# Value products in whole float32, the two heads of a pair on two column halves of the array

## The chip, the cores and the metric

The kernel runs on one core of a Trainium2 chip. The metric is the device time of one execution in microseconds (us). The engines are named as in the profile: PE (matrix products), PEld (its loads of the stationary operand), DVE (VectorE), ACT (ScalarE), POOL (GpSimd) and SP (SyncE, which issues the transfers).

## The reference

An attention with a threshold is followed by a gated MLP. B = 8 batches, H = 8 heads, S = 576 tokens, D = 64; the model width is 512, the MLP's inner width 1024.

```python
scores = scale * np.matmul(q, k.transpose(0, 1, 3, 2))
thresh = np.max(scores, axis=-1, keepdims=True) - tau
scores = np.where(scores >= thresh, scores, -1000000000.0)
attn = np.exp(scores - np.max(scores, axis=-1, keepdims=True))
attn = attn / (np.sum(attn, axis=-1, keepdims=True) + 1e-09)
x = np.matmul(attn, v)              # heads side by side: (B, S, 512)

h = gelu_tanh(x @ w_in)             # (B, S, 1024)
u, v = h[..., :512], h[..., 512:]
v_n = layer_norm(v) * g_ln
v_s = np.einsum('ts,bsd->btd', w_sg, v_n) + b_sg[None, :, None]
out = x + (u * v_s) @ w_out
```

All of it is float32.

## The kernel before

A pair of heads is the unit of attention: `attention(n, g0)` for n = 0 to 31, four pairs to a batch. `moe(b, m0)` is the MLP of one batch, and its steps are laid between those of the next batch's attention. The 576 tokens are four tiles of 128 and a tail of 64.

For one pair, nine tiles of scores are computed (four for each head, one with the tails of both). Each tile goes through the row maximum (`nm`, DVE, L771), the exponential (`exp`, ACT, L797), the selection by the threshold with the row sum (`stt`, DVE, L804), and four transposes on PE (`t`, L495), because the value products need the key tokens on the partitions. The query tokens are handled in two parts `p`, of 256 and 320 columns (`PARTS`).

Most products take both operands as a sum of two parts in the short format fp32r (hi and lo), which PE multiplies in one pass. For the value products of pairs n >= 4 this means:

- the transposed probabilities are copied out of their bank as `pth` by ACT (step `hi`, L886), and DVE subtracts that from the bank to get `ptl` (step `lo`, L892); the tails likewise (`thi` L911, `tlo` L918);
- the values are split by ACT (`v_hi`, L718) and POOL (`v_lo`, L722) into `vst`, in which the 128 columns of a weight tile hold the 64 hi and the 64 lo columns of one head;
- per head and part, `values_main` (steps `pva`, `pvb`, L933) and `values_tail` (`pvt`, `pvc`, L942) multiply five key tiles, each with hi and with lo, into a bank of their own;
- ACT copies the two halves of that bank out (`vl0`, `vl1`, L957 and L958), POOL adds them (`xadd`, L963) and multiplies by the reciprocal row sum (`rmul`, L971).

For the first four pairs (`WHOLE_VALUES = 4`, `whole_v` in the code) the values and probabilities are not split: the products run on float32 operands, with 128 weight columns that hold both heads' values, of which one half of the result is used (L955). The profile shows a float32 product as two instructions.

The result `x` is split into `xh` and `xl` for the MLP (`xh` ACT L975, `xl` POOL L979). The MLP's products are in `products` (L1050): `v`, `u`, `y` (the token mixing), `o`.

The order of all engines' work is one list. The kernel's body is first rehearsed by a `Planner`, which gives each operation a duration (`time_of`), simulates the engines, and writes the list. Each kind of step has a place in time, `OFF` and `START`, by which the planner chooses among the steps that could start. `LOOK` says per engine how far ahead it looks. Four PSUM banks (`b0` to `b3`) are given out by it as well; the scores have buffers of their own.

Of the kernel before, what the change touches and what calls it, by code (L numbers as in the profile page):

```python
# [20 lines left out]
P = 128  # L21
# [12 lines left out]
    tau=-10.43, q_tails=35.82, w_load=93.12, w_abs=-193.45, w_word=-6.26, w_mul=289.27, w_add=-517.97, w_hi=490.97,  # L34
    w_lo=88.35, w_cast=112.5, w_rest=110.21, w_place=-69.47, q_load=-19.53, q_scale=259.5, q_hi=-6.99, q_lo=142.39,
    q_place=-47.78, q_place_lo=-48.53, k_load=-7.75, k_hi=-106.32, k_lo=-457.88, k_place0=-35.09, k_place1=52.53,
    l_place0=5.62, l_place1=117.11, v_load=92.53, v_hi=397.22, v_lo=13.94, s=-1.81, nm=590.35, thr=-183.16,
    exp=181.68, stt=24.69, t=1.61, hi=2.32, lo=468.05, rep=76.71, tt=-25.16, thi=-43.36, tlo=71.94, guard=-110.37,
    recip=463.46, irep=-433.54, turn=-94.76, inv=154.09, pva=-176.92, pvt=-141.14, vl0=0.73, pvb=-23.65, pvc=1.45,
    vl1=63.24, xadd=-45.27, rmul=6.15, xh=629.7, xl=-44.57, pe=3.02, mcopy=10.33, msq=22.97, stt1=-7.91, tanh=4.97,  # L40
    stt2=-9.02, bn=17.0, ag=17.81, var=29.8, rstd=-93.73, shift=-18.7, vn=-147.62, z=-102.8, zh=-53.93, zl=-85.64,
    mg=-72.27, mgh=31.11, mgl=-83.38, mo=12.11, mxl=8.52, mxh=40.16, mst=6.76,
)
START = {
# [5 lines left out]
}  # L50
LAST_SCALE, SIGMA, SPREAD = 0.55, 1.155, 0.7
LOOK = dict(tensor=139.2, vector=19.4, scalar=59.9, gpsimd=0.0, sync=204.7)
# [3 lines left out]
WHOLE_SCORES, WHOLE_VALUES = 1, 4  # L56
# [22 lines left out]
def time_of(engine, op, out, args):  # L79
# [7 lines left out]
    if engine == "tensor":  # L87
        passes = 2 if op == "transpose" else 4 if args[0].dtype == F32 else 1
        return n * passes / (CLOCK if passes > 1 else STREAM) + 2
# [294 lines left out]
def tile_threshold_attention_gated_mlp(  # L384
# [21 lines left out]

    nc = tc.nc
# [76 lines left out]
    VB = 5 * P  # L484
    vst = cpool.tile([P, 2 * (VB + D)], F32R, name="vst")
    nc.gpsimd.memset(vst[D:P, NM * P:VB].bitcast(F32), 0.0)
    nc.gpsimd.memset(vst[0:D, VB + NM * P:2 * VB].bitcast(F32), 0.0)

# [123 lines left out]
    def attention(n, g0):  # L612
# [5 lines left out]
        whole_s, whole_v = n < WHOLE_SCORES, n < WHOLE_VALUES  # L618

        def load(name, src, w):  # L620
            if name == "v" and whole_v:
                pool, width, tag = xpool, S, f"x{'hl'[n % 2]}{4 + n // 2}"
            elif name != "v" and whole_s:
# [77 lines left out]
        def v_parts():  # L701
            r = st["v"]
            main = r[:, :2 * NM * D].rearrange("p (t h d) -> p h t d", t=NM, h=2)
            hi = vst[:, 0:2 * (VB + D)].rearrange("p (h x) -> p h x", h=2)[:, :, 0:NM * P]
            hi = hi.rearrange("p h (t x) -> p h t x", t=NM)[:, :, :, 0:D]
            lo = vst[:, D:D + 2 * (VB - D)].rearrange("p (h x) -> p h x", h=2)[:, :, 0:NM * P]
            lo = lo.rearrange("p h (t x) -> p h t x", t=NM)[:, :, :, 0:D]
            for h in range(2):
                yield main[:, h], hi[:, h], lo[:, h]
            for h in range(2):  # L710
                rows = slice(h * D, (h + 1) * D)
                o = h * VB + NM * P
                yield (r[rows, 2 * NM * D:S], vst[rows, o + h * D:o + h * D + D],
                       vst[rows, o + (1 - h) * D:o + (1 - h) * D + D])

        def v_hi():
            for src, hi, _ in v_parts():
                nc.scalar.activation(hi, src, AF.Copy)  # L718

        def v_lo():  # L720
            for src, hi, lo in v_parts():
                nc.gpsimd.tensor_tensor(lo, src, hi, ALU.subtract)  # L722

        def v_tail_room():
            t = st["vt"] = ptp.tile([P, P], F32, tag="ttl", name=f"vt{n}")
            for h in range(2):
                nc.gpsimd.memset(t[h * D:(h + 1) * D, (1 - h) * D:(2 - h) * D], 0.0)

        def v_tail():
            for h in range(2):  # L730
                rows = slice(h * D, (h + 1) * D)
                nc.scalar.activation(st["vt"][rows, rows], st["v"][rows, 2 * NM * D:S], AF.Copy)
# [118 lines left out]
        parts = [("h", F32)] if whole_v else [("h", F32R), ("l", F32R)]  # L851

        def unit(h, p):
            if ("u", h, p) not in st:
                st["u", h, p] = tuple(
                    ptp.tile([P, NM, S - 2 * P], dt, tag=f"pt{x}{h}", name=f"pt{x}{n}_{h}_{p}") for x, dt in parts)
            return st["u", h, p]

        def tail_unit(p):
            if ("tu", p) not in st:  # L860
                st["tu", p] = tuple(
                    ptp.tile([P, S - 2 * P], dt, tag=f"tt{x}", name=f"tt{x}{n}_{p}") for x, dt in parts)
            return st["tu", p]
# [9 lines left out]
        def views(h, i):  # L873
            tp = st["t", h, i]
            if i < NM:
                p, j = divmod(i, 2)
                cs = slice(j * P, (j + 1) * P)
                return [(tp.rearrange("p (k x) -> p k x", k=NM), *(x[:, :, cs] for x in unit(h, p)))]
            src = tp.rearrange("p (k h x) -> p h k x", k=NM, h=2)
            cs = slice(2 * P, 2 * P + TAIL)  # L880
            return [(src[:, hh], *(x[:, :, cs] for x in unit(hh, 1))) for hh in range(2)]

        def hi_parts(h, i):
            def f():
                for src, hi, *_ in views(h, i):
                    nc.scalar.activation(hi, src, AF.Copy)  # L886
            return f

        def lo_parts(h, i):
            def f():  # L890
                for src, hi, lo in views(h, i):
                    nc.vector.tensor_tensor(lo, src, hi, ALU.subtract)  # L892
# [15 lines left out]
        def tail_hi(i):  # L908
            def f():
                p, cs, w = tail_place(i)  # L910
                nc.scalar.activation(tail_unit(p)[0][:, cs], st["tt", i][:, 0:w], AF.Copy)  # L911
            return f

        def tail_lo(i):
            def f():
                p, cs, w = tail_place(i)
                hi, lo = tail_unit(p)
                nc.vector.tensor_tensor(lo[:, cs], st["tt", i][:, 0:w], hi[:, cs], ALU.subtract)  # L918
            return f

        def value_tile(h, kt):

            if whole_v:
                return st["v"][:, kt * P:(kt + 1) * P] if kt < NM else st["vt"]
            return vst[:, h * VB + kt * P:h * VB + (kt + 1) * P]

        def values_main(h, p):
            def f():
                w = PARTS[p][1]
                acc = st["acc", h, p] = bank(f"pv{n}_{h}_{p}")  # L930
                for kt in range(NM):
                    for x, part in enumerate(unit(h, p)):
                        nc.tensor.matmul(acc[:, 0:w], value_tile(h, kt), part[:, kt, 0:w],  # L933
                                         start=(kt == 0 and x == 0), stop=False)
            return f

        def values_tail(h, p):
            def f():
                w = PARTS[p][1]
                tail = tail_unit(p)  # L940
                for x, part in enumerate(tail):
                    nc.tensor.matmul(st["acc", h, p][:, 0:w], value_tile(h, NM), part[:, 0:w],  # L942
                                     start=False, stop=(x == len(tail) - 1))
            return f

        def low_values(h, p):
            def f():
                w = PARTS[p][1]
                mine, other = slice(h * D, (h + 1) * D), slice((1 - h) * D, (2 - h) * D)
                if ("x", p) not in st:  # L950
# [360 lines left out]
```

## Time and profile before

| | |
|---|---|
| median of 3 runs | 1072.83 us (1068.9 to 1073.52) |
| profiled execution: its own time | 1072.98 us |
| profiled execution: span of its instructions | 1071.2 us |
| PE busy | 1012.8 us, 95% of the span, 6972 instructions |
| PEld busy | 934.3 us, 87% |
| DVE busy | 812.3 us, 76% |
| ACT busy | 815.5 us, 76% |
| POOL busy | 764.5 us, 71% |
| mean granted PE clock | 0.989 |
| transfers | 95.45 MB |

Busy time is the time in which an engine has at least one instruction under way. A product is pipelined: its own duration is longer than the step from its start to the next start, so the pace of PE is read from starts. In lists of groups a row reads: line, engine, operation, output<-inputs, shape, count, then busy time in us and mean duration in ns, then the idle time before the group and what ended it. In lists of waits a row reads: the waiting engine and line, what released it, then us in total, how many times, the longest.

### The profile page before, as it was taken

The numbers are of one execution on the slowest core, as the hardware profiler recorded it, in microseconds if no ns is written. First come the engines' busy times: TensorE is split into PE (matmuls) and PEld (weight loads), VectorE is DVE, ScalarE is ACT, GpSimd is POOL, SyncE is SP. The second block draws the span as 40 slices with busy tenths as digits, with TensorE's granted clock in tenths as the row PEclk, the third lists the DMA queues.
The fourth block names the chain that finished last, engine by engine and source line by source line (L and its number), as shares of the span: only waits on it lengthen the run. The fifth ranks groups of instructions, "written<-read, shape, count | busy, mean of one in ns | idle before, by whom it ended". The sixth has DMA issues, their size and how long they took to land.

```text
span 1071.2 us, 21247 instructions
## 1 busy us (share of the span) xinstructions
PE 1012.8 (95%) x6972; PEld 934.3 (87%) x6972; DVE 812.3 (76%) x1755; ACT 815.5 (76%) x1849; POOL 764.5 (71%) x1331
## 2 busy tenths in 40 slices
PE   4888899999999999999999999999999999999998
PEld 2667777998989988998989998999889999899987
DVE  5775778787887878887787878788787887878450
ACT  4777778877887788878787778878787788977662
POOL 6877767657975688757876588747886578864766
PEclk9898999999999999999999999999999999999999
DMA  9453332334232433334323442334333343331101
GB/s 287 132 134 87 86 71 55 93 93 113 66 98 69 102 94 91 81 81 103 100 63 92 98 108 65 98 82 109 82 83 92 87 104 91 76 86 24 40 1 45
DMA packets 50767, 95.45 MB, mean 89 GB/s; under 512 B 8033, under 2 KB 16225, under 8 KB 50658
## 3 DMA queue, kind: packets, MB, share of 16 engines
q1 hardware_dynamic: 50658, 94.10, 34.2%
q8 instruction: 56, 0.92, 0.4%
q14 instruction: 53, 0.43, 0.1%
HBM read 37.39 MB, written 9.44 MB: 44 GB/s over the span
## 4 chain that ended last, share of the span: by engine, by line
PE 60%; ACT 14%; POOL 10%; DVE 8%; DMA 4%; issue 3%; SPq 0%; POOLq 0%; DVEq 0%; ACTq 0%
PE pv L933 12%; PE y L1050 11%; PE s L762 10%; PE u L1050 6%; PE t L495 6%; PE v L1050 5%; PE o L1050 4%; ACT p L797 3%; ACT pth L886 3%; PE pv L942 3%; PE t_i L495 2%; DVE ptl L892 2%; ACT vv L1126 2%; DVE p L804 1%; POOL ot L1230 1%
## 5 line engine op out<-in xcount | busy, mean ns | idle before, releaser
L804 DVE SCALAR_TENSOR_TENSOR p<-s,nm,p 128x576 f32<-128x576 f32 x256 | 204.7, 813 | 56.7 <-ACT p L797 37.0
L771 DVE TENSOR_REDUCE nm<-s 128x1 f32<-128x576 f32 x288 | 212.0, 747 | 44.3 <-PE s L762 43.5
L797 ACT ACTIVATE p<-s,nm 128x576 f32<-128x576 f32 x256 | 185.3, 745 | 36.0 <-DVE nm L771 34.1
L762 PE MATMUL s<-ks,qst 128*128 128x288 f32 x620 | 189.0, 323 | 8.2 <-DVE p L804 6.0
L892 DVE TENSOR_TENSOR ptl<-t,pth 128x512 fp32r<-128x512 f32 x280 | 169.4, 629 | 28.7 <-ACT pth L886 25.6
L886 ACT ACTIVATE pth<-t 128x512 fp32r<-128x512 f32 (+3 forms) x320 | 167.2, 558 | 26.0 <-PE t L495 24.7
L762 PE MATMUL s<-klz,qst 128*128 128x288 f32 x620 | 173.4, 296 | 0.0
L495 PE MATMUL t<-ident_r,p 128*128 128x128 f32 x1024 | 153.2, 278 | 1.9 <-DVE ptl L892 1.4
L495 PEld LDWEIGHTS t<-ident_r,p 128*128 128x128 f32 x1024 | 124.3, 143 | 8.2 <-DVE ptl L892 2.9
L762 PEld LDWEIGHTS s<-ks,qst 128*128 128x128 f32 x620 | 118.0, 190 | 15.4 <-DVE p L804 8.0
L933 PE MATMUL pv<-ptl,vst 128*128 128x256 f32 (+1 forms) x448 | 124.7, 301 | 4.5 <-DVE ptl L892 4.4
L933 PE MATMUL pv<-pth,vst 128*128 128x256 f32 (+1 forms) x448 | 126.4, 303 | 0.3 <-DVE uu L1033 0.3
L762 PEld LDWEIGHTS s<-klz,qst 128*128 128x128 f32 x620 | 118.3, 191 | 0.4
L777 POOL TENSOR_TENSOR nm<-columns,nm 128x1 f32<-128x1 f32 x288 | 56.8, 200 | 81.3 <-DVE nm L771 74.2
L1050 PE MATMUL y<-wsh,z 128*128 128x288 f32 (+2 forms) x512 | 112.3, 298 | 1.1 <-DVE uu L1033 0.7
L933 PEld LDWEIGHTS pv<-ptl,vst 128*128 128x128 f32 x448 | 84.6, 189 | 8.6 <-DVE ptl L892 7.7
L1050 PEld LDWEIGHTS y<-wsh,z 128*128 128x128 f32 x512 | 84.8, 188 | 1.7 <-DVE uu L1033 1.2
L933 PEld LDWEIGHTS pv<-pth,vst 128*128 128x128 f32 x448 | 84.5, 189 | 0.8 <-ACT pth L886 0.5
L1050 PE MATMUL o<-gl,woh 128*128 128x288 f32 (+2 forms) x256 | 76.8, 300 | 3.4 <-POOL gl L1202 2.9
L1050 PE MATMUL o<-gh,woh 128*128 128x288 f32 (+2 forms) x256 | 79.2, 309 | 0.3
L1050 PE MATMUL u<-xh,wih 128*128 128x288 f32 (+2 forms) x256 | 77.8, 304 | 0.0
L1050 PE MATMUL u<-xh,wil 128*128 128x288 f32 (+2 forms) x256 | 77.6, 303 | 0.0
(244 smaller groups left out, 2870.8 us busy)
## 6 DMA issues: line engine op xcount, KB each, us to landing
rk<-in_kT SPq DMA_DIRECT2D x32, 320.0 KB, 3.0
ks<-khi SPq DMA_DIRECT2D x62, 160.0 KB, 2.6
rq<-in_qT SPq DMA_DIRECT2D x32, 288.0 KB, 2.8
rv<-in_vP SPq DMA_DIRECT2D x32, 288.0 KB, 2.8
qst<-qhi SPq DMA_DIRECT2D x62, 144.0 KB, 2.4
qst<-rq SPq DMA_DIRECT2D x62, 144.0 KB, 2.4
ks<-khi SPq DMA_DIRECT2D x62, 144.0 KB, 2.5
out_T<-ot SPq DMA_DIRECT2D x56, 144.0 KB, 2.3
```

The costliest lines, as they stand in the source:

```text
L495: nc.tensor.transpose(out, x, ident_r.bitcast(F32))
L762: nc.tensor.matmul(sc[:, a, 0:HALF], w, x, start=(j == 0), stop=(j == len(terms) - 1))
L771: nc.vector.tensor_reduce(nmax, st["s", h, i][:, :, 0:HALF], AX.XY, ALU.max, negate=True)
L777: nc.gpsimd.tensor_tensor(thr, toff, st["nm", h, i], ALU.subtract)
L797: nc.scalar.activation(target(h, i), st["s", h, i][:, :, 0:HALF], AF.Exp, bias=st["nm", h, i])
L804: nc.vector.scalar_tensor_tensor(dst, st["s", h, i][:, :, 0:HALF], st["thr", h, i], dst, ALU.is_ge, ALU.mult, accum_out=st["l", p][:, c:c ...
L886: nc.scalar.activation(hi, src, AF.Copy)
L892: nc.vector.tensor_tensor(lo, src, hi, ALU.subtract)
L933: nc.tensor.matmul(acc[:, 0:w], value_tile(h, kt), part[:, kt, 0:w], start=(kt == 0 and x == 0), stop=False)
L942: nc.tensor.matmul(st["acc", h, p][:, 0:w], value_tile(h, NM), part[:, 0:w], start=False, stop=(x == len(tail) - 1))
L1050: nc.tensor.matmul(st["acc"], *term(j), start=(j == 0), stop=(j == n - 1))
L1126: nc.scalar.activation(st["v", i], st["v", i], AF.Identity, bias=t[:, 9:10], scale=t[:, 8:9])
```

## The change

All 32 pairs multiply the values in float32 whole. The two heads of a pair write to the two partition halves of one bank: head h has 64 weight columns and its result at partitions 64h to 64h + 63, so that the two heads' products stand on two column halves of the array. In the list of products the heads alternate within each key tile. Parts and steps that served the split values go (`v_hi`, `v_lo`, `lo`, `tlo`, the two copies `vl0` and `vl1`, `xadd`). The division by the row sum reads the bank directly and moves from POOL to DVE. The transposed probabilities have a float32 buffer for each head and part. The values come with their tail tile padded with zeros to 128 columns on the way in, into two buffers of their own. The planner's duration of a product with fewer than 128 output partitions and fewer than 512 columns is halved, plus 20 ns instead of 2; all places in `OFF` and `START` and the values of `LOOK` are replaced.

```diff
...
-LOOK = dict(tensor=139.2, vector=19.4, scalar=59.9, gpsimd=0.0, sync=204.7)
-WHOLE_SCORES, WHOLE_VALUES = 1, 4
+LOOK = dict(tensor=36.5, vector=4.6, scalar=95.7, gpsimd=0.0, sync=1009.1)
+WHOLE_SCORES = 1
...
-        return n * passes / (CLOCK if passes > 1 else STREAM) + 2
+        beside = 0.5 if out.shape[0] < P and n < 512 else 1.0
+        return n * passes * beside / (CLOCK if passes > 1 else STREAM) + (2 if beside == 1 else 20)
...
-        whole_s, whole_v = n < WHOLE_SCORES, n < WHOLE_VALUES
+        whole_s = n < WHOLE_SCORES
...
-            if name == "v" and whole_v:
-                pool, width, tag = xpool, S, f"x{'hl'[n % 2]}{4 + n // 2}"
+            if name == "v":
+                pool, width, tag = raws, KW, f"v{n % 2}"
...
-        at("v_load", g0, load("v", vP[b, hp], S))
-        if whole_v:
-            at("v_lo", g0, v_tail_room)
-            at("v_hi", g0, v_tail)
-        else:
-            at("v_hi", g0, v_hi)
-            at("v_lo", g0, v_lo)
+        at("v_load", g0, load("v", vP[b, hp], KW))
...
-                st["u", h, p] = tuple(
-                    ptp.tile([P, NM, S - 2 * P], dt, tag=f"pt{x}{h}", name=f"pt{x}{n}_{h}_{p}") for x, dt in parts)
+                st["u", h, p] = ptp.tile([P, NM, S - 2 * P], F32, tag=f"pt{h}{p}", name=f"pt{n}_{h}_{p}")
...
+        def values(p):
+
+            def f():
+                w = PARTS[p][1]
+                acc = st["acc", p] = bank(f"pv{n}_{p}")
+                for kt in range(NM + 1):
+                    for h in range(2):
+                        o = kt * P + h * D
+                        nc.tensor.matmul(acc[h * D:(h + 1) * D, 0:w], st["v"][:, o:o + D],
+                                         unit(h, p)[:, kt, 0:w] if kt < NM else tail_unit(p)[:, 0:w],
+                                         start=(kt == 0), stop=(kt == NM))
+            return f
...
-                    nc.gpsimd.tensor_tensor(x, x, st["ir", p][:, 0:w], ALU.mult)
+                    nc.vector.tensor_tensor(x, st["acc", p][:, 0:w], st["ir", p][:, 0:w], ALU.mult)
...
-            at("pva", g, values_main(0, p))
-            at("pvt", g, values_tail(0, p))
-            at("vl0", g, low_values(0, p))
-            at("pvb", g, values_main(1, p))
-            at("pvc", g, values_tail(1, p))
-            at("vl1", g, low_values(1, p))
-            if not whole_v:
-                at("xadd", g, add_values(p))
+            at("pv", g, values(p))
...
-    vt = vv[:, :, :, main:].reshape(b, h // 2, 2 * (s - main), d)
-    vP = np.concatenate([vm.reshape(b, h // 2, P, -1), vt], axis=3)
+    vt = np.zeros((b, h // 2, 2, s - main, 2, d), v.dtype)
+    for i in range(2):
+        vt[:, :, i, :, i] = vv[:, :, i, main:]
+    vP = np.concatenate([vm.reshape(b, h // 2, P, -1), vt.reshape(b, h // 2, P, P)], axis=3)
```

More of the change, by code (lines that the diff above doesn't have):

```diff
@@ L33 @@
 OFF = dict(
[L34 to L42, printed above, removed]
+    tau=-59.03, q_tails=21.54, w_load=93.25, w_abs=14.97, w_word=-11.36, w_mul=305.89, w_add=-53.25, w_hi=76.95,
+    w_lo=-29.06, w_cast=41.6, w_rest=284.92, w_place=-9.14, q_load=-28.85, q_scale=-26.89, q_hi=-25.56, q_lo=294.35,
+    q_place=54.06, q_place_lo=441.36, k_load=-20.12, k_hi=-120.23, k_lo=133.17, k_place0=51.8, k_place1=-202.5,
+    l_place0=-46.8, l_place1=-82.04, v_load=144.01, s=-26.3, nm=606.52, thr=-103.33, exp=57.84, stt=-13.0, t=35.7,
+    hi=-11.74, rep=71.62, tt=-54.0, thi=44.63, guard=-68.79, recip=-4.38, irep=52.78, turn=200.87, inv=-39.64,
+    pv=27.51, rmul=79.08, xh=-18.12, xl=3.72, pe=272.45, msq=234.54, stt1=-29.3, tanh=114.86, stt2=-21.69, bn=-93.0,
+    ag=-20.61, var=3.77, rstd=35.02, shift=-72.34, vn=49.38, z=-135.63, zh=-72.66, zl=37.97, mg=58.9, mgh=29.83,
+    mgl=187.71, mo=-46.37, mxl=-39.26, mxh=-54.09, mst=-58.62,
 )
 START = {
[5 rows of a table removed]
[5 rows of a table added]
 }
 LAST_SCALE, SIGMA, SPREAD = 0.55, 1.155, 0.7
-LOOK = dict(tensor=139.2, vector=19.4, scalar=59.9, gpsimd=0.0, sync=204.7)
-WHOLE_SCORES, WHOLE_VALUES = 1, 4
+LOOK = dict(tensor=36.5, vector=4.6, scalar=95.7, gpsimd=0.0, sync=1009.1)
+WHOLE_SCORES = 1
 Step = namedtuple("Step", "time kind fn group scale")
@@ L483, in tile_threshold_attention_gated_mlp @@
     nc.gpsimd.memset(pm[0:D, S:KW], 0.0)
[L484 to L487, printed above, removed]
     zt1 = cpool.tile([P, FH], F32R, name="zt1")
@@ L617, in attention @@
         lead = g0 - TILES
-        whole_s, whole_v = n < WHOLE_SCORES, n < WHOLE_VALUES
+        whole_s = n < WHOLE_SCORES
         def load(name, src, w):
-            if name == "v" and whole_v:
-                pool, width, tag = xpool, S, f"x{'hl'[n % 2]}{4 + n // 2}"
-            elif name != "v" and whole_s:
+            if name == "v":
+                pool, width, tag = raws, KW, f"v{n % 2}"
+            elif whole_s:
                 pool, width, tag = kpool, w, "ks00" if name == "q" else "ks10"
@@ L699, in attention @@
             at("l_place1", lead, k_place_lo(1))
[L701 to L732, printed above, removed]
-        at("v_load", g0, load("v", vP[b, hp], S))
-        if whole_v:
-            at("v_lo", g0, v_tail_room)
-            at("v_hi", g0, v_tail)
-        else:
-            at("v_hi", g0, v_hi)
-            at("v_lo", g0, v_lo)
+        at("v_load", g0, load("v", vP[b, hp], KW))
         def scores(h, i):
@@ L849, in spread_inverse @@
             return f
-        parts = [("h", F32)] if whole_v else [("h", F32R), ("l", F32R)]
         def unit(h, p):
             if ("u", h, p) not in st:
-                st["u", h, p] = tuple(
-                    ptp.tile([P, NM, S - 2 * P], dt, tag=f"pt{x}{h}", name=f"pt{x}{n}_{h}_{p}") for x, dt in parts)
+                st["u", h, p] = ptp.tile([P, NM, S - 2 * P], F32, tag=f"pt{h}{p}", name=f"pt{n}_{h}_{p}")
             return st["u", h, p]
@@ L860, in tail_unit @@
             if ("tu", p) not in st:
-                st["tu", p] = tuple(
-                    ptp.tile([P, S - 2 * P], dt, tag=f"tt{x}", name=f"tt{x}{n}_{p}") for x, dt in parts)
+                st["tu", p] = ptp.tile([P, S - 2 * P], F32, tag=f"tt{p}", name=f"tt{n}_{p}")
             return st["tu", p]
@@ L877, in views, with place @@
                 cs = slice(j * P, (j + 1) * P)
-                return [(tp.rearrange("p (k x) -> p k x", k=NM), *(x[:, :, cs] for x in unit(h, p)))]
+                return [(tp.rearrange("p (k x) -> p k x", k=NM), unit(h, p)[:, :, cs])]
             src = tp.rearrange("p (k h x) -> p h k x", k=NM, h=2)
             cs = slice(2 * P, 2 * P + TAIL)
-            return [(src[:, hh], *(x[:, :, cs] for x in unit(hh, 1))) for hh in range(2)]
-        def hi_parts(h, i):
+            return [(src[:, hh], unit(hh, 1)[:, :, cs]) for hh in range(2)]
+        def place(h, i):
             def f():
[L885 to L892, printed above, removed]
+                for src, dst in views(h, i):
+                    nc.scalar.activation(dst, src, AF.Copy)
             return f
@@ L906, in tail_place, with place_tail @@
             return p, slice(j * P, j * P + w), w
-        def tail_hi(i):
+        def place_tail(i):
             def f():
                 p, cs, w = tail_place(i)
-                nc.scalar.activation(tail_unit(p)[0][:, cs], st["tt", i][:, 0:w], AF.Copy)
+                nc.scalar.activation(tail_unit(p)[:, cs], st["tt", i][:, 0:w], AF.Copy)
             return f
[L914 to L927, printed above, removed]
+        def values(p):
             def f():
                 w = PARTS[p][1]
[L930 to L934, printed above, removed]
-            return f
@@ L937, in values_tail @@
[L937 to L950, printed above, removed]
-                    st["x", p] = xtmp.tile([P, S - 2 * P], F32, tag="x32", name=f"x32_{n}_{p}")
-                    if not whole_v:
-                        st["y", p] = xtmp.tile([P, S - 2 * P], F32, tag="y32", name=f"y32_{n}_{p}")
-                if whole_v:
-                    nc.scalar.activation(st["x", p][mine, 0:w], st["acc", h, p][mine, 0:w], AF.Copy)
-                    return
-                nc.scalar.activation(st["y", p][mine, 0:w], st["acc", h, p][mine, 0:w], AF.Copy)
-                nc.scalar.activation(st["x", p][mine, 0:w], st["acc", h, p][other, 0:w], AF.Copy)
-            return f
@@ L961, in add_values @@
-        def add_values(p):
-            w = PARTS[p][1]
-            return lambda: nc.gpsimd.tensor_tensor(
-                st["x", p][:, 0:w], st["x", p][:, 0:w], st["y", p][:, 0:w], ALU.add)
+                acc = st["acc", p] = bank(f"pv{n}_{p}")
[5 more added lines that the diff above has]
+                                         start=(kt == 0), stop=(kt == NM))
@@ L968, in f @@
                 c0, w = PARTS[p]
+                if what == 0:
+                    st["x", p] = xtmp.tile([P, S - 2 * P], F32, tag="x32", name=f"x32_{n}_{p}")
                 x = st["x", p][:, 0:w]
                 if what == 0:
-                    nc.gpsimd.tensor_tensor(x, x, st["ir", p][:, 0:w], ALU.mult)
+                    nc.vector.tensor_tensor(x, st["acc", p][:, 0:w], st["ir", p][:, 0:w], ALU.mult)
                 elif what == 1:
@@ L990, in attention @@
             at("t", g, transposes(h, i))
-            at("hi", g, hi_parts(h, i))
-            if not whole_v:
-                at("lo", g, lo_parts(h, i))
+            at("hi", g, place(h, i))
             if (h, i) in ((1, 0), (1, 1), (1, 2), (0, 3), (0, NM)):
@@ L997, in attention @@
                 at("tt", g, tail_transposes(i))
-                at("thi", g, tail_hi(i))
-                if not whole_v:
-                    at("tlo", g, tail_lo(i))
+                at("thi", g, place_tail(i))
         for p, t in ((0, 3), (1, 8)):
@@ L1007, in attention @@
             at("inv", g, spread_inverse(p))
-            at("pva", g, values_main(0, p))
-            at("pvt", g, values_tail(0, p))
-            at("vl0", g, low_values(0, p))
-            at("pvb", g, values_main(1, p))
-            at("pvc", g, values_tail(1, p))
-            at("vl1", g, low_values(1, p))
-            if not whole_v:
-                at("xadd", g, add_values(p))
+            at("pv", g, values(p))
             at("rmul", g, finish(p, 0))
@@ L1160, in new @@
                     if "uu" not in st:
-                        st["uu"] = ptp.tile([P, NM, S - 2 * P], F32, tag="pth0", name=f"uu{b}")
+                        st["uu"] = ptp.tile([P, NM, S - 2 * P], F32, tag="pt01", name=f"uu{b}")
                     st["u", p, d] = st["uu"][:, d, :]
@@ L1188, in gated @@
                     if ("gg", x) not in st:
-                        st["gg", x] = ptp.tile([P, NM, S - 2 * P], F32R, tag=f"pt{x}1", name=f"g{x}{b}")
+                        st["gg", x] = ptp.tile([P, NM, S - 2 * P], F32R, tag="pt11" if x == "h" else "pt00", name=f"g{x}{b}")
                     return st["gg", x][:, d, :]
```

10 rows, old and new, of the table START are left out of this document.

## The prediction

> **What bounds the kernel now.** I read the page's head first, then the windows by stage, then who waits for whom on the matmul engine (PE), then the chain of the opening.
>
> ```profile
> span 1071.2 us, 21247 instructions
> PEclk9898999999999999999999999999999999999999
> PE pv L933 12%; PE y L1050 11%; PE s L762 10%; PE u L1050 6%; PE t L495 6%; PE v L1050 5%; PE o L1050 4%; ACT p L797 3%; ACT pth L886 3%; PE pv L942 3%; PE t_i L495 2%; DVE ptl L892 2%; ACT vv L1126 2%; DVE p L804 1%; POOL ot L1230 1%
> ```
>
> The line of the chain that ended last has the value products (`pv`, lines 933 and 942) as its largest item, 15% of the span. By stage (columns: length, then PE, weight loads, DVE, ACT, POOL busy with counts, clock, DMA):
>
> ```profile
> 0.00:31.00 31.00, 16.02 (x43) 9.53 (x44) 19.73 (x37) 15.53 (x28) 22.64 (x42) 1.00 0.83 261
> 31.00:140.00 109.00, 93.99 (x481) 76.28 (x480) 77.12 (x145) 79.39 (x174) 79.79 (x123) 0.91 0.41 109
> 140.00:1010.00 870.00, 847.93 (x6088) 797.46 (x6087) 694.99 (x1530) 693.96 (x1593) 621.33 (x1114) 1.00 0.34 85
> 1010.00:1071.20 61.20, 54.83 (x366) 51.07 (x364) 20.52 (x44) 26.64 (x56) 40.70 (x54) 0.97 0.07 25
> ```
>
> Four stages. 0 to 31 us is loading. 31 to 140 is the opening: pairs of heads 0 to 3, whose values are already multiplied as whole float32, beside the splitting of the weights. 140 to 1010 is the steady part: PE busy 847.9 of 870 us, every other engine at 80% or less. After 1010 comes the last MLP. So in the steady part PE's own work is the time, and only 22 us there are PE idle; in the opening PE idles 15 of 109 us, at a granted clock of 0.91. What PE waits for:
>
> ```profile
> PE t_t L495 <- DVE p L804: 7.1, 6, 2.4
> PE pv L933 <- DVE ptl L892: 4.4, 7, 0.7
> PE t L495 <- DVE ptl L892: 1.4, 2, 0.7
> PE v L1050 <- ACT x L958: 0.9, 1, 0.9
> ```
>
> The first row is from the opening alone, the others from the steady part.
>
> **The price of the value products.** From the chain in order of time (start, us, what), first two f32r units of the steady part, then whole float32 ones of the opening, then those ones' group, then the opening's shares by line:
>
> ```profile
> 309.24 0.95 PE pv L933 x8
> 327.74 1.17 PE pv L933 x8
> ...
> 95.20 1.73 PE pv L933 x8
> 111.95 2.16 PE pv L933 x8
> 81.71 4.08 PE pv L933 x8
> ...
> L933 PE MATMUL pv<-pth,rv 128*128 128x256 f32 (+1 forms) x128 | 38.7, 451 | 0.5 <-ACT pth L886 0.5
> ...
> by line: PE pv L933 20.3%; PE s L762 9.2%; DMA w<-in_w_sgT 6.6%; DMA qst<-qhi 6.0%; ACT p L797 5.3%; issue 4.9%; DMA w<-in_w_in 4.9%; ACT pth L886 4.8%; PE pv L942 4.5%; PE t L495 3.7%; DVE p L804 2.9%; POOL wsl L572 2.0%; PE t_i L495 1.7%;
> ```
>
> A split f32r product takes 0.95/8 = 0.119 us at 256 columns and 1.17/8 = 0.146 at 320. A pair of heads has 2 heads x 5 key tiles x (hi, lo) = 20 of each width: 20 x 0.119 + 20 x 0.146 = 5.30 us. A whole float32 product is two instructions (the trace has 128 `pv<-pth,rv` where the code has 64), each 1.73/8 = 0.216 and 2.16/8 = 0.270 us. Ten products, so 20 instructions, of each width: 9.72 us per pair of heads, serially.
>
> After the change all 32 pairs issue these same 20 + 20 instructions, each with 64 weight columns, heads alternating between the column halves. What it costs is one question: does head 1's instruction stream beside head 0's? In order of issue head 0's second instruction must wait for its first (same half), but head 1's first can run beside it, and so on down the list, so the order allows full overlap. The trace has no two products on different halves, so I bound it.
> - Full overlap, each at the float32 row's own pace: 9.72/2 = 4.86 us per pair of heads.
> - The two streams share what limits f32r: two times 256 columns at 0.119 each is 0.238 for a pair of instructions, and 0.292 at 320; 10 x 0.238 + 10 x 0.292 = 5.30 us, exactly the split price.
> - No overlap: 9.72 us.
>
> I take the middle of the first two, 5.08 us: the pair's streams together ask for 512 columns in 0.216 us against f32r's 512 in 0.238, 10% more than any row here shows, and nothing shows either way whether the halves share it. Steady part: 28 x (5.08 - 5.30) = -6 us, ends -12 and 0. Opening: 4 x (5.08 - 9.72) = -18.6 us of PE work; there `pv` is 20.3 + 4.5% of the chain, and one group ran at 4.08 instead of 2.16 (lowered clock), so the work is on the path. But DVE, ACT and POOL are at 71 to 73% of that stage, and a chain through `w_sgT` loads stands there too; with 12 us gone their 77 to 80 us of work would stand at 79 to 82% of 97 us, the level of the steady part. I count two thirds, -12 us, ends -19 and 0.
>
> The Trainium skill, "TensorE: Matmul & The Clock Gate", Part 3, states that matmuls on distinct column groups run concurrently, each further tile adding some 4 ns, and gives 2.38x measured for three column tiles. No run here shows it. By the 4 ns the pair would cost 4.86 + 20 x 0.004, about 4.9 us (an estimate); by 2.38/3 for two tiles, 1.59x, it would be 9.72/1.59 = 6.1 us, and the sum about no change at all.
>
> **Weight loads and switching.** The nearest rows are the last token tile's products, 64 weight columns on one half:
>
> ```profile
> 1026.11 0.39 PE L1050 MATMUL v<-wih,xl 128*128 128x512 f32 x1
> 1026.34 0.40 PE L1050 MATMUL v<-wih,xh 128*64 128x512 f32 x1
> 1026.58 0.39 PE L1050 MATMUL v<-wil,xh 128*64 128x512 f32 x1
> ...
> 1028.87 0.39 PE L1050 MATMUL v<-wih,xl 128*64 128x512 f32 x1
> 1029.10 0.30 PE L1050 MATMUL u<-xh,wih 128*128 128x320 f32 x1
> ...
> L1050 PEld LDWEIGHTS v<-wih,xh 128*128 128x128 f32 x128 | 24.1, 188 | 6.0 <-DVE ptl L892 1.7
> L1050 PEld LDWEIGHTS v<-wih,xh 128*64 128x64 f32 x32 | 4.3, 134 | 3.5 <-ACT x L958 1.1
> ```
>
> The load of 64 columns takes 134 ns against 188, so 54 ns less; two of them per 0.216 to 0.27 us pair ask no more than one full load per 0.119 us product now, which is hidden. Starts step by 0.23 us into the 64-column group, inside it, and out of it: a switch costs nothing there. Price taken: 0; ends 0 and 0.16 us a switch (a product's 0.39 less its 0.23 step, the array emptying), with 64 units and two switches each, 128 x 0.16 = +20 us. It is one half alone, so it is not proof for two.
>
> **What leaves the other engines.**
>
> ```profile
> L892 DVE TENSOR_TENSOR ptl<-t,pth 128x512 fp32r<-128x512 f32 x280 | 169.4, 629 | 28.7 <-ACT pth L886 25.6
> L918 DVE TENSOR_TENSOR ttl<-t_t,tth 128x128 fp32r<-128x128 f32 (+1 forms) x140 | 37.7, 272 | 15.9 <-ACT tth L911 15.8
> L718 ACT ACTIVATE vst<-rv 128x256 fp32r<-128x256 f32 (+1 forms) x112 | 31.9, 334 | 6.3 <-PE pv L942 4.4 <-PE pv L933 1.4
> L957 ACT ACTIVATE y<-pv 64x256 f32<-64x256 f32 (+1 forms) x112 | 45.2, 403 | 29.0 <-PE pv L942 27.7
> L958 ACT ACTIVATE x<-pv 64x256 f32<-64x256 f32 (+1 forms) x112 | 45.5, 406 | 2.0
> L722 POOL TENSOR_TENSOR vst<-rv,vst 128x256 fp32r<-128x256 f32 (+1 forms) x112 | 56.6, 527 | 24.9 <-ACT vst L718 22.3
> L963 POOL TENSOR_TENSOR x<-x,y 128x256 f32<-128x256 f32 (+1 forms) x56 | 45.0, 803 | 21.5 <-ACT x L958 20.9
> L971 POOL TENSOR_TENSOR x<-x,ir 128x256 f32<-128x256 f32 x64 | 52.3, 818 | 5.6 <-ACT x L955 3.7
> ...
> L892 DVE TENSOR_TENSOR ptl<-t,pth 128x256 fp32r<-128x256 f32 x56 | 21.0, 417 | 5.1 <-ACT pth L886 4.5
> L1184 DVE SCALAR_TENSOR_TENSOR uu<-y,uu 128x320 f32<-128x320 f32 x4 | 1.9, 483 | 4.4 <-PE y L1050 4.4
> ```
>
> DVE loses 169.4 + 37.7 = 207 us and gains the division straight from the bank: 32 x (0.417 + 0.483) = 29 us, by the last two rows (same operands' places, same widths). ACT loses 31.9 + 45.2 + 45.5 = 123 us, POOL 56.6 + 45.0 + 52.3 = 154 us. Nearly all of it lies beside PE and is worth nothing by itself. On the path is the subtraction between a transpose's copy and the products (0.63 us later each time), which PE waits on for 4.4 + 1.4 us, and `x` for 0.9: 6.7 us. The copy itself stays and is late next, and other waits ease with lighter engines: I count -5 us. The numbers that place every step (`OFF`, `START`, `LOOK`) are replaced too, so the order of the whole list changes; no row can price that, and it stands against the 22 us of idle that the present order leaves: ends for waits and order together -10 and +5. The new DVE instruction waits for the products; behind it in DVE's queue stand the row maxima and selections that PE's transposes need (7.1 us above). DVE has 178 us more room for that and the bank is freed by one reader instead of two, so I price it at 0. The wider load of the values is as large as that of the keys:
>
> ```profile
> rk<-in_kT SPq DMA_DIRECT2D x32, 320.0 KB, 3.0
> rv<-in_vP SPq DMA_DIRECT2D x32, 288.0 KB, 2.8
> ```
>
> By these rows 0.2 us more each, 32 times, on DMA engines that are 34% busy in the steady part, and issued as early as before: 0. One bank in place of two per unit, and one buffer per head and part, take waits away only.
>
> **Sum.** The profiled execution took 1072.98 us (span 1071.2), beside a median of 1072.83, so no correction. 1073 - 12 (opening) - 6 (steady products) - 5 (waits) = 1050 us. All best ends: 1073 - 19 - 12 - 10 = 1032; all worst ones with overlap: 1078. The three ends are independent, so their distances from the middle are added as squares: down by the root of 7^2 + 6^2 + 5^2, 10.5, up by that of 12^2 + 6^2 + 10^2, 16.7: 1039 to 1067 is the forecast's own range.
>
> **Rivals.**
> - *The halves run one after the other* (the other side). Then each pair of heads costs 9.72 us: 28 x 4.42 = +124, opening unchanged, waits -5: 1192 us. For it: no row shows two products at once, and 64 columns alone step by the same 0.23 us as 128. Against it: the trace has no two products on different halves to show a conflict. It decides where a pair of instructions takes more than 1.2 times one: 28 x (x - 5.30) + (2/3) x 4 x (x - 9.72) - 5 = 0 gives x = 5.85 us per pair of heads, and 5.85/4.86 = 1.2. Chance 0.13.
> - *Overlap with a toll.* A drain of the array at each of the 128 changes between full and halved columns adds up to the 20 us above: 1070 us; overlap of only 1.6x gives about 1075. Against it: the 0.23 us steps into and out of the 64-column group. The Trainium skill, "TensorEngine Tiling (Array Packing)", Key Properties, says that changing the tiling mode drains the engine; the rows above show none, but with one tile in use. Chance 0.12.
> - *The opening doesn't shorten*, because the weights' chain and the other engines at 71 to 73% hold it, or the clock falls further when PE has less to do there: 1073 - 6 - 5 = 1062, or 1068 where the streams share as well. For it: `w_sgT`, `w_in` and `qst` loads are 17.5% of that chain; against it: `pv` is 24.8%. Chance 0.07.
>
> **Chances.** Forecast (full overlap, gain in the opening) 0.68. About 0.5% (5.4 us) is what a measurement of this kernel can tell from no change. Faster by more: 0.66 + 0.03 + 0.04 = 0.73. Within: 0.02 + 0.06 + 0.03 = 0.11. Slower: 0.13 + 0.03 = 0.16. The range 1030 to 1075 holds the forecast's case with its ends, the opening rival and most of the toll; serial halves are left out. Its low end is that of all best ends.
>
> **What would show it.** Right: `pv` instructions in pairs that start together, a unit of 20 taking some 2.2 us at 256 and 2.7 at 320 columns; the opening ending near 128 us; DVE near 634 us busy, ACT near 690, POOL near 610; PE still over 93%. Wrong: `pv` starts stepping by 0.216 (serial); a gap of 0.1 us or more at every unit's first product or at the transpose behind it (toll); PE idle over 25 us between 31 and 130 us (opening); PE waiting on the new DVE division.

## The result, and the profile after

The changed kernel takes 1039.66 us (median; 1037.77 to 1041.02) against 1073.09: a ratio of 0.9696, 95% interval 0.9667 to 0.9724, so 3.0% faster. The forecast was 1050 us in a range of 1030 to 1075.

The head of the changed kernel's page (busy time, share of the span, instructions):

```profile
span 1039.2 us, 20206 instructions
PE 982.1 (95%) x6972; PEld 842.6 (81%) x6972; DVE 654.9 (63%) x1399; ACT 699.8 (67%) x1489; POOL 617.5 (59%) x1089
```

DVE, ACT and POOL lost 157, 116 and 147 us; PE, which sets the time, lost 31 at the same number of products. The windows by stage are cut at the end of the fourth pair's last value product and at that of the last one of all (length, then PE, PEld, DVE, ACT, POOL busy, clock, DMA). First the kernel before, cut in that way, then the changed one:

```profile
31.00:139.97 108.97, 93.96 (x481) 76.25 (x480) 77.12 (x145) 79.38 (x174) 79.76 (x123) 0.91 0.41 109
139.97:1008.95 868.98, 846.91 (x6082) 796.44 (x6079) 694.99 (x1530) 693.13 (x1592) 620.53 (x1113) 1.00 0.34 85
1008.95:1071.20 62.25, 55.88 (x374) 52.12 (x372) 20.52 (x44) 27.48 (x57) 41.53 (x56) 0.98 0.07 25
```

```profile
29.00:127.40 98.40, 78.43 (x480) 60.39 (x479) 71.78 (x143) 72.13 (x150) 70.01 (x102) 0.86 0.46 127
127.40:975.80 848.40, 831.30 (x6076) 719.86 (x6076) 543.56 (x1175) 587.22 (x1263) 488.47 (x897) 1.00 0.34 88
975.80:1039.20 63.40, 56.38 (x378) 52.78 (x376) 21.08 (x45) 26.95 (x56) 40.43 (x54) 0.97 0.07 25
```

The opening ends 12.6 us earlier (139.97 to 127.40), the steady part is 20.6 us shorter, the last MLP 1.2 us longer: 32.0 us, the difference of the spans. Of the 12.6 us, 1.9 lie ahead of the first value product, which starts at 29.47 instead of 31.35 us. PE's idle time in the steady part goes from 22.1 to 17.1 us; in the opening it grows from 15.0 to 20.0.

One value unit of the changed kernel in the timeline (start, us, what), with its neighbours:

```profile
336.92 0.29 PE L719 MATMUL s<-ks,qst 128*128 128x288 f32 x1
337.05 0.29 PE L719 MATMUL s<-klz,qst 128*128 128x288 f32 x1
337.27 1.95 PE L869 MATMUL pv<-pt,rv 128*64 128x256 f32 x16
339.05 0.60 PE L869 MATMUL pv<-tt,rv 128*64 128x256 f32 x4
339.58 0.40 PE L949 MATMUL y<-wsh,z 128*128 128x288 f32 x1
339.82 0.29 PE L949 MATMUL y<-wsl,z 128*128 128x288 f32 x1
339.95 0.29 PE L949 MATMUL y<-wsh,z 128*128 128x288 f32 x1
```

Sixteen instructions take from 337.27 to 339.05, 1.78 us; before, eight whole float32 ones on the full array took 1.73. In the single records the two heads' instructions start 6 to 7 ns apart and the next pair 0.216 us after (0.269 at 320 columns): the halves overlap fully, at the pace of one float32 product alone. But the unit has edges. A score product's next start normally comes 0.133 us later; here it comes at 337.27 instead of 337.18, and the first pair takes 0.05 us longer: 0.14 us in. Ten pairs at 0.216 would end at 337.27 + 0.05 + 2.16 = 339.48; `y` starts at 339.58, and its second product comes 0.24 instead of 0.133 us later: 0.20 us out, together some 0.345 us. I call it the toll. 61 of the 64 units show it; the other three, in the opening, ran at a lowered clock (0.40 to 0.48 us from pair to pair). The way in is 0.14 us at every neighbour. But 47 units are left through a transpose, and counted to the second product behind it the way out is then 0.16 us, so 0.30 a unit (the rows of the run with the f32r product of 64 columns, below, show one such end). With 17 units at 0.345 the toll is about 20 us in all, 17.5 of them in the steady part (42 units at 0.30, 14 at 0.345).

### The profile page after: what moved, and what is told of

It is laid out like the page before. It is cut to its first block, busy times and chain, and to the rows that moved or that the text cites. A ratio compares the mean times of both kernels' runs of the same rounds, so it can differ in the third digit from the quotient of the medians.

```text
span 1039.2 us, 20206 instructions
## 1 busy us (share of the span) xinstructions
PE 982.1 (95%) x6972; PEld 842.6 (81%) x6972; DVE 654.9 (63%) x1399; ACT 699.8 (67%) x1489; POOL 617.5 (59%) x1089
## 5 line engine op out<-in xcount | busy, mean ns | idle before, releaser
L761 DVE SCALAR_TENSOR_TENSOR p<-s,nm,p 128x576 f32<-128x576 f32 x256 | 206.8, 815 | 133.3 <-ACT p L754 81.4
L754 ACT ACTIVATE p<-s,nm 128x576 f32<-128x576 f32 x256 | 188.5, 746 | 28.4 <-DVE nm L728 27.3
L839 ACT ACTIVATE pt<-t 128x512 f32<-128x512 f32 (+1 forms) x320 | 164.9, 556 | 25.3 <-PE t L491 24.4
L491 PE MATMUL t<-ident_r,p 128*128 128x128 f32 x1024 | 148.5, 281 | 1.6 <-DVE x L881 0.9
L869 PE MATMUL pv<-pt,rv 128*64 128x320 f32 (+1 forms) x1024 | 140.7, 417 | 0.5 <-ACT pt L839 0.5
L719 PEld LDWEIGHTS s<-ks,qst 128*128 128x128 f32 x620 | 122.7, 198 | 20.1 <-issue 10.4
L491 PEld LDWEIGHTS t<-ident_r,p 128*128 128x128 f32 x1024 | 124.5, 145 | 7.2 <-DVE x L881 2.1
L869 PEld LDWEIGHTS pv<-pt,rv 128*64 128x64 f32 x1024 | 69.7, 138 | 51.0 <-issue 8.5
L858 ACT ACTIVATE tt<-t_t 128x128 f32<-128x128 f32 (+1 forms) x160 | 42.0, 267 | 51.8 <-PE t_t L491 47.7
L949 PE MATMUL o<-gh,woh 128*128 128x288 f32 (+2 forms) x256 | 76.2, 298 | 0.0
L949 PE MATMUL u<-xl,wih 128*128 128x288 f32 (+2 forms) x256 | 76.0, 297 | 0.0
L949 PE MATMUL y<-wsl,z 128*128 128x288 f32 (+2 forms) x256 | 75.4, 294 | 0.0
```

The source lines that it names most:

```text
L491: nc.tensor.transpose(out, x, ident_r.bitcast(F32))
L719: nc.tensor.matmul(sc[:, a, 0:HALF], w, x, start=(j == 0), stop=(j == len(terms) - 1))
L754: nc.scalar.activation(target(h, i), st["s", h, i][:, :, 0:HALF], AF.Exp, bias=st["nm", h, i])
L761: nc.vector.scalar_tensor_tensor(dst, st["s", h, i][:, :, 0:HALF], st["thr", h, i], dst, ALU.is_ge, ALU.mult, accum_out=st["l", p][:, c:c ...
L839: nc.scalar.activation(dst, src, AF.Copy)
L858: nc.scalar.activation(tail_unit(p)[:, cs], st["tt", i][:, 0:w], AF.Copy)
```

## The experiments

All ratios are against the kernel before, measured on the same chip beside each run. Where a time is set against the changed kernel's 1039.66 us, the two were not run side by side; by the ratios these differences come out the same within 3 us.

**The two heads one after the other.** The loops of `values` are exchanged:

```diff
-                for kt in range(NM + 1):
-                    for h in range(2):
+                for h in range(2):
+                    for kt in range(NM + 1):
```

> The changed kernel, with the products of a unit in another order: all five key tiles of head 0, then those of head 1, so that neighbours use the same column half. Same instructions, same list of steps. If the two halves run beside each other in the changed kernel (my theory), each pair of heads now pays 4.86 us more: 28 x 4.86 = 136 us in the steady part and up to 19 in the opening, 1040 + 140 to 155 = 1180 to 1195 us, and starts step by 0.216 and 0.270 us. If the pairs that start 7 ns apart in the trace were only recorded so and did not run together, the time stays near 1040.

Measured: 1126.0 us, ratio 1.0504 (1.0477 to 1.0531): 86 us slower than the changed kernel. The overlap is real, but the price is not the expected one; the time lies between the two that were named. The steady part of this run, then one of its units:

```profile
133.70:1062.70 929.00, 915.90 (x6078) 771.73 (x6077) 547.32 (x1173) 585.40 (x1262) 488.87 (x898) 1.00 0.31 80
170.76 2.00 PE L869 MATMUL pv<-pt,rv 128*64 128x256 f32 x10
172.54 0.38 PE L869 MATMUL pv<-tt,rv 128*64 128x256 f32 x1
172.60 0.38 PE L869 MATMUL pv<-pt,rv 128*64 128x256 f32 x1
172.75 0.38 PE L869 MATMUL pv<-tt,rv 128*64 128x256 f32 x1
172.81 1.24 PE L869 MATMUL pv<-pt,rv 128*64 128x256 f32 x5
173.89 0.59 PE L869 MATMUL pv<-tt,rv 128*64 128x256 f32 x2
```

In program order head 0 has eight `pt` and two `tt` instructions, and only then come head 1's eight and two. Here ten `pt` start before the first `tt`: in the single records head 1's first starts 6 ns behind head 0's seventh, while three of head 0's are still to come, and its row runs beside them. All 64 units have this order. From first to last start the unit takes 3.345 us, not 4.10 (20 x 0.216 less one), and 4.145 at 320 columns, so by the steps between starts 1.345 + 1.665 = 3.01 us more per pair of heads than in the changed kernel (2.000 and 2.480). 28 x 3.01 = 84 us; the steady part measured 929.0 - 848.4 = 80.6 us longer. The Trainium skill, "TensorE: Matmul & The Clock Gate", Part 3, says that matmuls start and end strictly in program order; this run shows products on the other column half starting ahead of it.

**The same in the opening alone** (pairs n < 4).

> The changed kernel with that serial order for the first four pairs of heads alone; 19.4 us more PE work in the opening. If PE's value products set the length of the opening (my theory), +12 to +19 us: 1052 to 1059. If the weights' chain or the other engines set it, +0 to +5: 1040 to 1045.

Measured: 1045.27 us, ratio 0.9758 (0.9736 to 0.9780), 5.6 us over the changed kernel, 6.6 by the ratios: between the two expected ranges, and nearer to the one in which other work sets the opening. But with the reordering just seen the edit adds not 19.4 but 4 x 3.01 = 12.0 us of PE work. Its opening and its steady part:

```profile
29.00:135.40 106.40, 88.39 (x479) 64.56 (x478) 74.34 (x145) 73.37 (x150) 71.63 (x104) 0.90 0.45 120
135.40:979.50 844.10, 828.96 (x6077) 718.27 (x6076) 541.90 (x1173) 586.57 (x1262) 488.43 (x897) 1.00 0.34 88
```

The opening is 8.0 us longer than 98.40, and the steady part gives 4.3 of them back. In the run before this, with the same edit in the opening, the fourth pair's products end at 133.7 us, 6.3 later than in the changed kernel. So half to two thirds of PE's added value work in the opening lengthens it, near the two thirds that the prediction counted; the granted clock there moves too (0.86, here 0.90), so this share is rough.

**The old places** (`OFF`, `START`, `LOOK` of the kernel before).

> The changed kernel with the places of the kernel before (OFF, START, LOOK; the one value step gets the place of the first of the old ones). If the gain comes from what is computed where (my theory), the time stays within 10 us of the changed kernel: 1040 to 1050. If a good part of the steady part's gain comes from the new order, 1055 or more.

Measured: 1128.94 us, ratio 1.0541 (1.0516 to 1.0566). My theory falls: the new steps need their own places. The steady part is 920.3 us long and PE idles 60.5 of them, against 17.1 in the changed kernel. PE's longest waits in this run:

```profile
PE t_t L492 <- DVE p L762: 38.6, 23, 5.7
PE s L720 <- DVE p L762: 13.3, 9, 3.7
PE s L720 <- DVE pm L762: 10.9, 4, 6.9
```

The same structure can cost 1040 or 1129 us by its order. So a change of structure that is given a new list can't be read without places that fit it, and the next two runs show the same.

**A DVE operation between copy and products again**, first as steps of their own with the old subtraction's places and a list made anew, then with the changed kernel's list kept. The second's edit, whose condition leaves the operation out of the planner's rehearsal (the tails likewise):

```diff
                     nc.scalar.activation(dst, src, AF.Copy)
+                    if not isinstance(tc, Planner):
+                        nc.vector.tensor_tensor(dst, src, dst, ALU.max)
```

> The changed kernel with a DVE operation of the size of the old subtraction put back between the copy of the transposes and the products (the maximum of the bank and its own copy, so that the values stay), 207 us of DVE work, on the products' path as before. If the short stalls that went from the steady part were due to that subtraction (my theory), 15 to 27 us come back: 1055 to 1067. If they went with the lighter ACT and POOL, or with the new places, +0 to +6: 1040 to 1046.

> The changed kernel with a DVE operation of the old subtraction's size (maximum of the bank and its copy) put behind each copy of the transposes, with the list of steps kept as it is. 207 us more DVE work, and the products wait 0.6 us longer for their operands. If that work was what stalled PE (my theory): +15 to +27, 1055 to 1067, with PE waits on the new operation. If it was ACT and POOL: +0 to +6. Above 1075 it would say that DVE's queue, which the list fills for its own load, holds PE in other places than before.

Measured: 1142.77 us (ratio 1.0667, 1.0638 to 1.0695) and 1197.47 us (1.1171, 1.1140 to 1.1202). The first is far beyond both expected ranges, the second is in the case above 1075 that its expectation named; neither sizes the subtraction. The second's trace fits that case: the added operation stands in DVE's queue and waits, while PE waits for another DVE operation, the selection:

```profile
DVE pt L841 <- ACT pt L839: 75.3, 155, 1.8
PE t_t L491 <- DVE p L761: 50.6, 31, 5.1
```

The first is confounded as the old places are.

**One part alone, in the kernel before, its list kept.** First the subtractions go (they stay in the planner's rehearsal alone), then also ACT's second copy and POOL's addition. `twice` gives the products the hi part in place of the lo part, so these kernels leave out the low parts of the probabilities, the second also those of half the values:

```diff
-                    nc.vector.tensor_tensor(lo, src, hi, ALU.subtract)
+                    if isinstance(tc, Planner):
+                        nc.vector.tensor_tensor(lo, src, hi, ALU.subtract)
...
-                    for x, part in enumerate(unit(h, p)):
+                    for x, part in enumerate(twice(unit(h, p))):
```

> The kernel before, same list of steps, same number and size of products, without the DVE subtractions (ptl and its tails); the products take the hi part twice, so the low parts of the probabilities are left out. It does one part of the change alone. If the short stalls that went from the steady part were due to that subtraction (my theory), 15 to 27 us go: 1045 to 1057. If they went with ACT's and POOL's work or with the new list, 0 to 6 us: 1066 to 1073.

> The kernel before without the DVE subtractions and also without ACT's second copy out of the product banks (y, 45 us) and POOL's addition (45 us); list of steps, number and size of products kept. The low parts of probabilities and of half the values are left out. Without the subtractions alone it was 1059.6 us. If ACT's and POOL's work on that path stalled PE as well (my theory for the rest of the steady gain): 1045 to 1053. If the rest came with the new list: 1056 to 1060.

Measured: 1059.62 us, ratio 0.9891 (0.9874 to 0.9908), and 1054.87 us, ratio 0.9861 (0.9848 to 0.9875). Their steady parts, with 20 products of each width per pair of heads as before:

```profile
137.40:996.00 858.60, 838.41 (x6082) 794.88 (x6080) 522.30 (x1110) 692.26 (x1592) 618.87 (x1114) 1.00 0.35 86
138.40:991.00 852.60, 834.99 (x6082) 794.48 (x6081) 523.13 (x1110) 654.25 (x1481) 576.91 (x1058) 1.00 0.35 87
```

The subtraction alone was worth 869.0 - 858.6 = 10.4 us, between the 15 to 27 expected and the 0 to 6 of the other case; the copy and the addition, both off PE, another 6.0 us in these profiles. The whole runs differ by 4.8 us (3.2 by the ratios), with intervals that touch, so the second size is rough.

**The toll, put in the middle of a unit.** One product of 64 rows by some columns, into unused columns of the bank, three times: f32r with 128 columns, f32r with 64, float32 with 64. The first run's edit:

```diff
                 for kt in range(NM + 1):
+                    if kt == 2 and not isinstance(tc, Planner):
+                        nc.tensor.matmul(acc[:, 384:448], ident_r, ident_r[:, 0:D], start=False, stop=False)
```

> The changed kernel with one small product of all 128 columns (64 wide, into unused columns of the same bank) in the middle of each value unit; list of steps kept. It doubles the changes between full and halved columns. In the trace a change in and out costs 0.14 + 0.20 us a unit. If that is the price of changing the column halves (my theory): 64 x 0.345 = 22 us and 2 us for the products, 1064. If it belongs to the start and end of a group in a bank: +2 to +5, 1042 to 1045.

> The same with a small product of 64 columns on head 0's half, so that no change of halves is added: +2 to +5 by my theory, 1042 to 1045; about +24 as in the run with full columns if any other product between costs as much.

> The changed kernel with one small product (64 wide, 64 columns on head 0's half) in the middle of each value unit, this time in float32, so of the same kind as its neighbours; list of steps kept. The run with the f32r product of 64 columns cost 16 us. If what costs is the change between products laid on the full array and on a column half, and an f32r product of 64 columns lies on the full array (my theory): 0 to +6 us against the changed kernel, 1040 to 1046. If any product that breaks the row of pairs costs it: about +16, 1056.

Measured: 1058.38, 1055.96 and 1044.77 us (ratios 0.9885, 0.9868 to 0.9902; 0.9860, 0.9840 to 0.9881; 0.9768, 0.9755 to 0.9782). Against the changed kernel that is 18.7, 16.3 and 5.1 us. The units from first to last start, at 256 columns: 2.379, 2.325 and 2.110 us against 2.000. The second run, then the third:

```profile
306.13 1.08 PE L871 MATMUL pv<-pt,rv 128*64 128x256 f32 x8
307.15 0.24 PE L868 MATMUL pv<-ident_r 128*64 128x64 f32 x1
307.32 1.08 PE L871 MATMUL pv<-pt,rv 128*64 128x256 f32 x8
308.24 0.60 PE L871 MATMUL pv<-tt,rv 128*64 128x256 f32 x4
308.77 0.33 PE L491 MATMUL t_t<-ident_r,p 128*128 128x128 f32 x1
308.86 0.38 PE L719 MATMUL s<-ks,qst 128*128 128x288 f32 x1
309.07 0.29 PE L719 MATMUL s<-klz,qst 128*128 128x288 f32 x1
```

```profile
306.56 1.08 PE L871 MATMUL pv<-pt,rv 128*64 128x256 f32 x8
307.47 0.22 PE L868 MATMUL pv<-both 128*64 128x64 f32 x1
307.48 0.43 PE L871 MATMUL pv<-pt,rv 128*64 128x256 f32 x1
307.53 0.22 PE L868 MATMUL pv<-both 128*64 128x64 f32 x1
307.59 1.03 PE L871 MATMUL pv<-pt,rv 128*64 128x256 f32 x7
```

An f32r product between the pairs costs the toll again (0.38 and 0.325 us a unit, its own streaming of 0.03 us included), whether it has 128 columns or 64. A float32 product of the same 64 columns slips in for its own streaming (0.05 us for each of its two instructions, 0.11 us a unit, 7 us in all), and head 1's instructions go on beside it. The expectation for f32r at 64 columns was a miss, and it is the key: such a product behaves like one on the full array.

A rival fits these three runs as well: that the change between the formats float32 and f32r is what costs. The opening of the kernel before rules it out, since there whole float32 products on the full array stand between f32r ones:

```profile
67.61 0.59 PE L942 MATMUL pv<-tth,vt 128*128 128x256 f32 x2
67.86 0.48 PE L762 MATMUL s<-ks,qst 128*128 128x288 f32 x1
68.18 0.30 PE L762 MATMUL s<-klz,qst 128*128 128x288 f32 x1
68.31 0.30 PE L762 MATMUL s<-ks,qst 128*128 128x288 f32 x1
68.45 0.29 PE L762 MATMUL s<-klz,qst 128*128 128x288 f32 x1
68.58 1.67 PE L933 MATMUL pv<-pth,rv 128*128 128x256 f32 x7
```

Two float32 instructions and one score product at their own paces (0.216, 0.216, 0.133) lead from 67.61 to 68.18, where the second score product starts; on the way back the first float32 instruction starts 0.13 us behind the last score product, and in the single records the next one 0.215 us later. Nothing is lost either way. A transpose, float32 on 128 columns, pays behind the halves too: its start comes 0.310 us after the unit's last pair's instead of 0.209, and from that pair to the second product behind the transpose (308.46 to 309.07 above) 0.61 us pass where the paces add up to 0.45. So the toll is that of a change between float32 products on column halves and products on the full array, among which an f32r product of 64 columns counts; why it does is open. The Trainium skill, "TensorEngine Tiling (Array Packing)", Key Properties, says that changing the tiling mode drains the engine; these runs agree that such a change costs time, 0.14 us in and 0.16 to 0.20 us out, and none of them shows the draining itself.

**The toll in the planner, and half as many changes.** In the first run the two prices replace the flat 20 ns of a product, and the places are searched anew with the planner's own list as the measure. In the second both parts of a pair of heads are also multiplied in one row of 40 instructions. Both have these lines:

```diff
+                    if ops[k][6] != halves[0]:
+                        start += 140 if ops[k][6] else 205
+                        halves[0] = ops[k][6]
```

> The changed kernel, with the price of a change between full array and column halves (0.14 us in, 0.205 us out) written into the planner in place of the flat 20 ns a product, and the places (OFF, START, LOOK) chosen anew for that by a search over the planner's list. Products, operations and buffers are the same. The toll itself stays, 64 x 0.345 = 22 us; what can go is idle and short stalls, of which the steady part has 29 us beside the toll: by my theory (the list matters, as the run with the old places showed) 8 to 15 us, 1025 to 1032. If the toll in the planner and new places bring nothing, 1038 to 1042.

> The same, but both parts of a pair of heads (256 and 320 columns) are multiplied in one row of 40 instructions at the pair's end, the first part's result in the free half of the bank of the reciprocals' transposes; places searched for this form. Half as many changes: 32 x 0.345 = 11 us less toll. Buffers and the bank are held longer, so the stalls may grow. If the toll decides (my theory as far as it goes): 1028 or less, below the run with the toll known; if the longer hold costs more than 11 us: 1032 to 1040.

Measured: 1062.90 us (ratio 0.9941, 0.9923 to 0.9959) and 1058.90 us (0.9888, 0.9869 to 0.9908). Both miss, and neither beats the changed kernel: places that a model likes need not fit the chip. PE waits 14.3 us at one place of the first run's start,

```profile
PE s L712 <- POOL rq L648: 14.3, 1, 14.3
```

and its steady part is 861.7 us long. The second is 4 us faster than the first with half the toll, but two lists differ as well, so this doesn't show that fewer changes pay.

## Why the prediction was right, step by step

- **Full overlap: right.** The pair runs at the float32 row's own pace, so the low end, 4.86 us per pair of heads, was the true one; the middle of 5.08 halved the gain. The term is 28 x (4.86 - 5.30) = -12.3 us, not -6.
- **Switches at 0: wrong.** The rival's toll came at its full size, about 20 us in all, +17.5 of them in the steady part; with it the value products there cost 5 us more than before (-12.3 + 17.5). The step that failed is the choice of the row: an f32r product of 64 columns beside f32r ones shows no change, since such a product counts as one on the full array.
- **Opening -12: right**, in size (12.6, of which 1.9 lie ahead of the value products) and in kind: PE is busy 15.5 us less there, and 5.0 of these turned into idle time. The tail transposes now wait 17.9 us for the selection on DVE (`PE t_t L491 <- DVE p L761`), where it was 7.1.
- **Waits -5: mis-sized.** The idle time did fall by 5.0 us, and the new division on DVE, priced at 0, holds PE for only 0.9. But -20.6 = -12.3 + 17.5 + the rest, and the rest is about -26 us of stalls (time beyond the products' own pace), most of which were never idle time in the profile. A product lasts 0.29 us in the records while its successor could start after 0.133, so a delay of up to 0.16 us is hidden in "busy". At each product's own pace (f32r 0.459 ns a column, a transpose 0.109 us, the value products as above) the steady part's products need 814 us before and 801 after; the excess is 55 us before, of which only 22 showed as idle, and 47 after, of which 17.5 are the toll. A unit of the kernel before in its timeline:

```profile
295.73 0.30 PE L933 MATMUL pv<-pth,vst 128*128 128x320 f32 x1
296.72 0.42 PE L933 MATMUL pv<-ptl,vst 128*128 128x320 f32 x1 [0.69 <-DVE ptl L892]
296.97 0.31 PE L933 MATMUL pv<-pth,vst 128*128 128x320 f32 x1
297.12 0.31 PE L933 MATMUL pv<-ptl,vst 128*128 128x320 f32 x1
```

The first step is 0.99 us instead of 0.146, 0.84 us lost; the row gives 0.69 as idle. The second is 0.25 instead of 0.146 and counts as busy. Of the 26 us, the runs without the subtractions and without copy and addition show 10.4 and about 6, if what they gained in the kernel before adds up here. The other 10 are not separated: the splitting of the values, the division, the buffers and the list went with them, and by the run with the old places the list alone can move far more than that.
- **The rivals.** Serial halves: refuted. The toll: true as a mechanism, outweighed by the stalls. An opening that doesn't shorten: refuted. The time given for an overlap of only 1.6x, about 1075, counts the whole opening; with the prediction's own two thirds it is 1073 + 22 - 10 - 5 = 1080.

Against the forecast the products saved 6 us more and the stalls 21 us more, and the toll, left out of the sum, took 17.5 back: the spans differ by 32 us where 23 were forecast (the medians by 33). So the overlap and the opening were foreseen, but that the time came within 10 us of the forecast is in part luck: the two largest errors, the toll and the stalls, nearly cancel. With the toll as found and the waits as counted it would have been 1073 - 12.6 - 12.3 + 17.5 - 5, about 1061.

## What to carry to other kernels

Two float32 products on the two column halves of the array run in the time of one, which makes whole float32 as cheap as hi and lo in f32r and takes the splitting off the other engines. Here the changes around the rows ate up what the products themselves saved in the steady part, and the gain there came from the stalls that went. Each change to other products and back costs about a third of a microsecond, which speaks for long rows of such products, though no run here gained by longer ones. Price PE stalls by the steps between starts against the pace of each kind of product, not by the profile's idle time, which here showed 22 of 55 us. And judge a new structure only with an order that fits it: the order alone moved this one by 89 us.

## What the runs showed of the hardware that was not expected

- Products on one column half start ahead of earlier ones that wait for the other half: head 1's first with three of head 0's still to start, in the run with the heads one after the other.
- A change from products on the full array to float32 products on column halves costs 0.14 us, the way back 0.16 us to a transpose and 0.20 us to other products. An f32r product of 64 columns counts as full for it; a change of format alone costs nothing.
- A small float32 product on one half leaves the other half's row going, and costs its own 0.05 us per instruction.
